# Two-layer attention kernel: value accumulators laid out by head and half of the queries

## The chip, the cores and the metric

One core of one Trainium2 chip runs the whole program. The metric is the device time of one execution in microseconds (us); the times shown are medians over several runs. The changed kernel does the same computation on the same inputs.

## What is computed

Two attention layers, A and B, are applied in turn, twice each, to one sequence of 2048 tokens of width 576, all in fp32. Both have 32 heads of 18 features; in A each head has keys and values of its own, in B all heads share one set.

```python
def _A_ref(x, wqkv, wo):
    qkv = ((x @ wqkv).reshape(B, S, 3, H, Dh)).transpose(2, 0, 3, 1, 4)
    q, k, v = qkv[0], qkv[1], qkv[2]
    scores = jnp.einsum("bhqd,bhkd->bhqk", q, k) * (Dh ** -0.5)
    p = _softmax(scores, axis=-1)
    o = jnp.einsum("bhqk,bhkd->bhqd", p, v)
    return o.transpose(0, 2, 1, 3).reshape(B, S, D) @ wo
# _B_ref: the same, with k and v of shape (B, S, Dh) shared by the heads
x = x + _A_ref(_layernorm(x), A_wqkv, A_wo)
x = x + _B_ref(_layernorm(x), B_wq, B_wk, B_wv, B_wo)
x = x + _A_ref(_layernorm(x), A_wqkv, A_wo)
x = x + _B_ref(_layernorm(x), B_wq, B_wk, B_wv, B_wo)
```

## The kernel before

A layer has a projection stage, a long stage of attention, and an output projection. Attention is worked in units: one pair of heads (p, 16 of them) by 512 queries (u, 4 of them), 64 units in a layer. Of a unit's 2048 keys, a head's scores are made twice.

First come the maxima. A matmul of kind "m" (line 653) gives the scores of 128 queries by 512 keys in a PSUM bank, and VectorE (DVE) reduces them (line 658). For four of the 32 in a unit the matmul takes the difference of two key blocks instead (kind "r", line 639), ScalarE (ACT) applies a relu (line 651), and DVE adds that while it reduces a later block (line 656), so that 28 reductions are left. The negated maxima go through GpSimd (POOL, lines 857 and 858), a DVE transpose (863) and DRAM (864, 868) into two rows of the query operand, so that the second score matmul has the maximum subtracted already.

Then come the exps. A matmul of kind "e" (line 879) gives 128 keys by 512 queries; ACT takes the exp into an SBUF tile `pt` (line 883). There are 32 in a unit, 16 of each head. The two heads of the pair lie on rows 0 to 63 and 64 to 127 of the array, so an "e", "m" or "r" of head 0 and one of head 1 can run side by side. All these matmuls share seven PSUM banks.

Last come the values. `pv_block` (line 913) multiplies four `pt` tiles, two key blocks of 128 by two heads, by the values: four matmuls with 19 columns of weights (18 features and a one, which gives the row sum) into four groups of 32 partitions of the one accumulator bank `oacc`, 512 queries wide. A group holds one head and either the even or the odd key blocks. A unit thus has 8 blocks of 512 columns, 4096 in all. fp32 makes two passes of each matmul.

When a unit's values are complete, ACT copies `oacc` to `oc` (line 930), and POOL adds the two key halves: `o_sum` (935) moves two groups and adds (939, 940) into `os`. Then the row sums are spread over 128 partitions by a DMA (`l_part`, 945), inverted on POOL (`l_inv`, 949), stored (`l_out`, 952), read back broadcast (`l_rows`, 957), multiplied on POOL (`o_mul`, 962) and the result is sent to `o_d` (`o_out`, 967). All DMAs go out on SyncE's queue (SP).

The order on TensorE (PE) in the steady stage is written out by hand in `UNIT` (line 70): ten phases of a unit. Each phase issues its rows in order ("e10" is kind, head and rank of the PSUM bank among the least recently used) and then a number of value columns, cut at block boundaries into segments. `PV_LAG` (line 81) says by how many columns the values trail: the first 928 columns of the first phases are left out. Maxima run 14 steps (`LEAD`; a step is four exps, an eighth of a unit) ahead of the exps, so 56 of a layer's 2048 maxima come before the loop of line 1044. After it the last exps go four by four (line 1060), with 512 value columns each, and parts of the output projection between.

The other steps of a unit are due at fixed distances, in steps, after its last exps (`SUM_AT` to `O_AT`, lines 50 to 57); `run_todo` issues what is due at the start of each phase.

Of the kernel before, what the change touches and what calls it, by code (L numbers as in the profile page):

```python
# [8 lines left out]
F32 = mybir.dt.float32  # L9
# [37 lines left out]
LEAD = 14  # L47
NM_AT = 2.5
ROW_AT = 5
SUM_AT = 3.75  # L50
L_AT = 5
INV_AT = 8
R_AT = 8
RB_AT = 11
MUL_AT = 13
O_AT = 15
SOON = (11.6, 12.6, 2.9)
FIRST = (8, 6)


# [6 lines left out]

UNIT = [("e00 m10 m02 e10 e01 e10 m00", 448),  # L70
# [9 lines left out]
UNIT = [([(o[0], int(o[1]), int(o[2])) for o in rows.split()], cols) for rows, cols in UNIT]  # L80
PV_LAG = 928
UNIT_M = [(kind, a) for rows, _ in UNIT for kind, a, _ in rows if kind != "e"]
assert len(UNIT_M) == 32 and sum(cols for _, cols in UNIT) == 4096

# [2 lines left out]
def tile_kernel(ctx: ExitStack, tc: tile.TileContext, A_x, A_wqkv, A_wo, B_x, B_wq, B_wk, B_wv, B_wo, out):  # L87
# [55 lines left out]
    r_d = dram.tile([H, S], F32, name="r_d")  # L143
    x_d = dram.tile([len(AWAY), P, D], F32, name="x_d")

    rb = cst.tile([P, 512], F32, name="rb")

    sums = [cst.tile([P, 512], F32, name=f"os{i}") for i in range(2)]

# [308 lines left out]
    for layer in range(4):  # L458
# [7 lines left out]
        def v_of(c):  # L466
            return vs[c // 8][:, c % 8] if is_a else vs[0][:, c]
# [113 lines left out]
                    fixed_rows(k_slot(p), True)  # L581
                load_rows(k_slot(p), D + 2 * p * DH, DH, 0, S, (i - 2,))

        mxs, nms, pts, ocs = {}, {}, {}, {}

        def ops(p):
            return big[:, q_slot(p)], big[:, k_slot(p)]
# [316 lines left out]
        def pv_cols(cols):  # L904

            while cols:
                n, c0 = divmod(pv_at[0], 512)
                w = min(cols, 512 - c0)
                pv_block(n, c0, c0 + w)
                pv_at[0] += w  # L910
                cols -= w

        def pv_block(n, c0, c1):

            p, u, i = *divmod(n // STEPS, 4), n % STEPS * 4
            cs = slice(c0, c1)
            turn[0] += 1
            for i in range(i, i + 4) if turn[0] % 2 else range(i + 3, i - 1, -1):
                a, kc = (i // 2) % 2, i // 4 * 2 + i % 2
                j = 64 * a + 32 * (kc % 2)  # L920
                nc.tensor.matmul(oacc[j:j + DH + 1, cs], v_of(kc)[:, 2 * p + a if is_a else 0, :], pts[p, u, i][:, cs],  # L921
                                 start=kc < 2 and c0 == 0, stop=kc >= 14 and c1 == 512)
                if c1 == 512:
                    pt = pts.pop((p, u, i))
                    free.extend(j for j, x in enumerate(ring) if x is pt)
            if c1 == 512 and i // 4 == STEPS - 1:
                oc = ocs[p, u] = ocs["tile"]
                ticks[0] += 1
                if m_done[0] < 4 * ns:
                    nc.scalar.activation(oc, oacc, AF.Copy)  # L930
                else:
                    copy(nc.vector, oc, oacc)


        def o_sum(p, u):
            oc = ocs.pop((p, u))
            t = sums[u % 2]
            for j in (0, 64):
                copy(nc.gpsimd, t[j:j + 32], oc[j + 32:j + 64])
            nc.gpsimd.tensor_tensor(t[:96], t[:96], oc[:96], op=OP.add)  # L940

        def l_part(p, u):
            lt = lts[p, u] = pool.tile([P, 8], F32, name="lt")
            for a in range(2):
                nc.sync.dma_start(lt[64 * a:64 * a + 64, :], sums[u % 2][64 * a + DH:64 * a + DH + 1, :])

        def l_inv(p, u):
            rl = rls[p, u] = pool.tile([P, 8], F32, name="rl")
# [5 lines left out]

        def l_rows(p, u):
            for a in range(2):
                nc.sync.dma_start(rb[64 * a:64 * a + DH, :],
                                  r_d[2 * p + a:2 * p + a + 1, u * 512:(u + 1) * 512].to_broadcast([DH, 512]))

        def o_mul(p, u):  # L960
            t = sums[u % 2]
            nc.gpsimd.tensor_tensor(t[:96], t[:96], rb[:96], op=OP.mult)  # L962

        def o_out(p, u):
            for a in range(2):
                c = (2 * p + a) * DH
                nc.sync.dma_start(o_d[c:c + DH, u * 512:(u + 1) * 512], sums[u % 2][64 * a:64 * a + DH, :])


        relu, raw = (pool.tile([P, 640], F32, tag="xh", bufs=2, name=n) for n in ("relu", "raw"))  # L970
# [17 lines left out]
        for p in range(NPAIR):  # L988
            for u in range(4):
                b = STEPS * (4 * p + u) + STEPS - 1  # L990
                if is_a or p or u:
                    at(b + NM_AT, max_store, p, u)
                    at(b + (SOON[2] if b == ns - 1 else ROW_AT), max_rows, p, u)
                soon = p == NPAIR - 1 and u == 0
                for d, f in ((SUM_AT, o_sum), (L_AT, l_part), (INV_AT, l_inv), (R_AT, l_out), (RB_AT, l_rows),
                             (SOON[0] if soon else MUL_AT, o_mul), (SOON[1] if soon else O_AT, o_out)):
                    at(b + LEAD + d, f, p, u)
            if p + 1 < NPAIR and is_a:
                for d, f in ((0, diff_in), (3, diff_split), (5, diff_out), (10 if p else 8, diff_rows)):
                    at(max(LEAD, 32 * p - 8) + d, f, p + 1)  # L1000
            if is_a and p in (0, 1):
                at(LEAD + 20 + 32 * p, load_rows, q_slot(p + 1), 2 * (p + 1) * DH, DH, 1536, S)
            if p + 1 < NPAIR:
                for i in range(4 if is_a else 2):
                    at(LEAD + 32 * (p - 1) + 1 + 8 * i if p else LEAD + 1 + 4 * i, load_part, p + 1, i)
# [15 lines left out]
                    f(*args)  # L1021

        b = LEAD + ns
        at(b - 9.75, out_rows, 0)
        at(b - 7, out_hi, 0, nc.vector)
        at(b - 6, out_lo, 0)
        at(b - 2, out_rows, 1)
        for i, (f, args) in enumerate(fill):
            if is_a and i % 8 == 0:
# [3 lines left out]
            f(*args)  # L1033
        assert not weave["left"] and m_done[0] == 4 * LEAD
        e_next = [0, 0]
        ocs["tile"] = ptile("oc")

        def exp_next(a, rank=0):
            pu, kc = divmod(e_next[a], NCH)
# [20 lines left out]
        while sum(e_next) < 4 * ns:  # L1060
            run_todo(LEAD + sum(e_next) / 4)
            for _ in range(min(4, 4 * ns - sum(e_next))):
                exp_next(int(e_next[0] > e_next[1]), next(i for i, j in enumerate(lru) if j not in held))
            left, c = 4 * ns - sum(e_next), -pv_at[0] % (512 * STEPS)
            if left < 4 * STEPS and 0 < c <= 512:
                pv_cols(c)
                for _ in range(FIRST[0]):
                    next(first)
                pv_cols(512 - c)
            else:  # L1070
                if left // 4 == 1:
                    for _ in range(FIRST[1]):
                        next(first)
                pv_cols(512)
        outs = out_proj(layer == 3, first)
        for st in range(ns, ns + L_AT + 1):
            run_todo(LEAD + st)
            if st < ns + OUT_AHEAD:
                next(outs)
                pv_cols(512 * ns - pv_at[0] - (0 if st > ns else 512))  # L1080
        tail = [todo.pop(n, []) for n in range(ns + LEAD + L_AT + 1, ns + LEAD + O_AT)]
        assert not todo, todo

# [30 lines left out]
```

## Time and profile before

| what | us |
|---|---|
| median of 3 runs | 5525.5 (5524.3 to 5525.83) |
| span of the profiled execution | 5520.9 |
| PE busy | 5509.2 |
| DVE busy | 4920.3 |
| ACT busy | 4889.3 |
| POOL busy | 1839.9 |
| weight loads (PEld) | 3050.7 |

Four layers follow one another, and each has about 1145 us of the steady stage. Busy times are unions of instructions: where instructions of one engine overlap, as ACT's, DVE's and PE's do here, a busy share near 100% does not say that the engine could do no more. What an engine could do is read from the time between the starts of two instructions that follow without a wait, and what bounds a stage from the time between the starts of its blocks.

### The profile page before, as it was taken

The numbers are of one execution on the slowest core, as the hardware profiler recorded it, in microseconds if no ns is written. First come the engines' busy times: TensorE is split into PE (matmuls) and PEld (weight loads), VectorE is DVE, ScalarE is ACT, GpSimd is POOL, SyncE is SP. The second block draws the span as 40 slices with busy tenths as digits, with TensorE's granted clock in tenths as the row PEclk, the third lists the DMA queues.
The fourth block names the chain that finished last, engine by engine and source line by source line (L and its number), as shares of the span: only waits on it lengthen the run. The fifth ranks groups of instructions, "written<-read, shape, count | busy, mean of one in ns | idle before, by whom it ended". The sixth has DMA issues, their size and how long they took to land.

```text
span 5520.9 us, 143086 instructions
## 1 busy us (share of the span) xinstructions
PE 5509.2 (100%) x55774; PEld 3050.7 (55%) x55774; DVE 4920.3 (89%) x9493; ACT 4889.3 (89%) x9882; POOL 1839.9 (33%) x2382
## 2 busy tenths in 40 slices
PE   9999999999999999999999999999999999999999
PEld 8655555454855555555686555545458545454546
DVE  4799999998799999999637999999977999999995
ACT  3599999999299999999626999999992999999996
POOL 3243333334233323233412433333342333333332
PEclk9999999999999999999999999999999999999999
DMA  6321111111411000001243211111114111010002
GB/s 219 119 60 45 45 45 48 43 45 34 136 57 31 24 24 21 24 21 25 64 176 109 58 49 43 45 46 48 40 43 133 54 28 25 24 25 21 24 15 84
DMA packets 277610, 306.04 MB, mean 55 GB/s; under 512 B 136434, under 2 KB 194378, under 8 KB 267642
## 3 DMA queue, kind: packets, MB, share of 16 engines
q1 hardware_dynamic: 276930, 296.89, 18.7%
q8 instruction: 437, 7.16, 0.5%
q14 instruction: 243, 1.99, 0.1%
HBM read 169.68 MB, written 123.13 MB: 53 GB/s over the span
## 4 chain that ended last, share of the span: by engine, by line
PE 97%; issue 1%; DVE 1%; ACT 1%; DMA 0%; POOL 0%; SPq 0%; POOLq 0%; ACTq 0%
PE oacc L921 38%; PE pse L879 27%; PE psm L653 17%; PE psn L275 7%; PE psq L481 5%; PE psm L639 3%; DVE mx L658 1%; ACT pt L883 1%; PE ps L261 0%; POOL ev L494 0%; DMA m_d<-tr 0%; DMA qk_d<-ev 0%; PE oacc L262 0%; DMA big<-m_d 0%; DMA big<-qk_d 0%
## 5 line engine op out<-in xcount | busy, mean ns | idle before, releaser
L883 ACT ACTIVATE pt<-pse 128x512 f32<-128x512 f32 x8192 | 4185.0, 612 | 10.1 <-PE pse L879 1.9
L658 DVE TENSOR_REDUCE mx<-psm 128x1 f32<-128x512 f32 x6208 | 3942.4, 684 | 88.6 <-PE psm L653 66.3
L879 PE MATMUL pse<-big 64*128 64x512 f32 x8192 | 2280.5, 432 | 0.5 <-DMA big<-m_d 0.5
L653 PE MATMUL psm<-big 62*128 62x512 f32 x7200 | 2158.9, 443 | 2.2 <-ACT evr L493 0.8
L879 PEld LDWEIGHTS pse<-big 64*128 64x128 f32 x8192 | 1174.4, 184 | 1064.2 <-ACT pt L883 758.2
L921 PE MATMUL oacc<-pt,vbuf 128*19 128x32 f32 (+11 forms) x26544 | 1728.2, 368 | 0.3 <-ACT oc L930 0.2
L653 PEld LDWEIGHTS psm<-big 62*128 62x128 f32 x7200 | 878.2, 184 | 204.3 <-DVE mx L658 75.9
L921 PEld LDWEIGHTS oacc<-pt,vbuf 128*19 128x19 f32 x26544 | 533.9, 98 | 819.9 <-issue 661.4
L186 POOL TENSOR_SCALAR hl<-neg 128x8 fp32r<-128x8 f32 x256 | 50.6, 198 | 2462.2 <-DVE neg L854 2462.2
L921 PE MATMUL oacc<-pt,vy 128*19 128x288 f32 (+3 forms) x8176 | 566.3, 383 | 0.0
L949 POOL TENSOR_TENSOR rl<-lt,mone 128x8 f32<-128x8 f32 x256 | 422.0, 1648 | 320.0 <-DMA lt<-os 318.1
L656 DVE CUSTOM_DVE_ANT_0 relu<-psm,relu 128x512 f32<-128x512 f32 x496 | 342.9, 691 | 76.3 <-ACT pt L883 50.9
L186 POOL TENSOR_SCALAR os<-oc 32x512 f32<-32x512 f32 x512 | 315.3, 616 | 102.4 <-DVE oc L186 50.6
L656 DVE CUSTOM_DVE_ANT_0 xo<-psm,xo 128x512 f32<-128x512 f32 x496 | 332.1, 670 | 15.5 <-ACT pt L883 1.6
L490 ACT ACTIVATE ev<-psq 128x512 fp32r<-128x512 f32 (+1 forms) x112 | 66.9, 597 | 311.5 <-PE psq L481 222.4
L940 POOL TENSOR_TENSOR os<-os,oc 96x512 f32<-96x512 f32 x256 | 330.6, 1291 | 21.4
L962 POOL TENSOR_TENSOR os<-os,rb 96x512 f32<-96x512 f32 x256 | 327.9, 1281 | 23.1 <-DMA rb<-r_d 23.1
L921 PEld LDWEIGHTS oacc<-pt,vy 128*19 128x19 f32 x8176 | 189.8, 98 | 242.0 <-issue 197.7
L651 ACT ACTIVATE xo<-psm 128x512 f32<-128x512 f32 x496 | 317.1, 639 | 0.0
L275 PE MATMUL psn<-wsm,xx 128*128 128x288 f32 x2240 | 310.4, 297 | 0.1
L275 PEld LDWEIGHTS psn<-wsm,xx 128*128 128x128 f32 x2240 | 299.0, 188 | 15.4 <-issue 13.1
L651 ACT ACTIVATE relu<-psm 128x512 f32<-128x512 f32 x496 | 303.6, 612 | 0.0
(102 smaller groups left out, 2781.3 us busy)
## 6 DMA issues: line engine op xcount, KB each, us to landing
big<-qk_d SPq DMA_DIRECT2D x172, 432.0 KB
qk_d<-ev SPq DMA_DIRECT2D x96, 512.0 KB
qk_d<-ev SPq DMA_DIRECT2D x120, 256.0 KB
rb<-r_d SPq DMA_DIRECT2D x512, 36.0 KB
o_d<-os SPq DMA_DIRECT2D x512, 36.0 KB
o<-o_d SPq DMA_DIRECT2D x56, 256.0 KB
xx<-qk_d SPq DMA_DIRECT2D x120, 72.0 KB
big<-m_d SPq DMA_DIRECT2D x512, 4.0 KB
```

The costliest lines, as they stand in the source:

```text
L186: eng.tensor_scalar(dst, src, 1.0, 0.0, op0=OP.mult, op1=OP.add)
L275: nc.tensor.matmul(ps, lhs[:, xc, :], wsm[:, wc, h * 288:(h + 1) * 288], start=i == 0, stop=i == len(TERMS) - 1)
L651: nc.scalar.activation(t, ps, AF.Relu)
L653: nc.tensor.matmul(ps, q[b:b + KM, c0:c0 + P], k[b:b + KM, kb * 512:(kb + 1) * 512], start=True, stop=True)
L656: nc.vector.tensor_tensor_reduce(t, ps, t, 1.0, LOWEST, OP.add, OP.max, mx[:, r:r + 1])
L658: nc.vector.reduce_max(mx[:, r:r + 1], ps, axis=AX.X)
L879: nc.tensor.matmul(e, k[r:r + KE, kc * P:(kc + 1) * P], q[r:r + KE, u * 512:(u + 1) * 512], start=True, stop=True)
L883: nc.scalar.activation(pt, e, AF.Exp, scale=SCALE)
L921: nc.tensor.matmul(oacc[j:j + DH + 1, cs], v_of(kc)[:, 2 * p + a if is_a else 0, :], pts[p, u, i][:, cs], start=kc < 2 and c0 == 0, stop=k ...
L940: nc.gpsimd.tensor_tensor(t[:96], t[:96], oc[:96], op=OP.add)
L949: nc.gpsimd.tensor_tensor(rl, lts.pop((p, u)), mone, op=OP.pow)
L962: nc.gpsimd.tensor_tensor(t[:96], t[:96], rb[:96], op=OP.mult)
```

## The change

The accumulator is divided otherwise: its four groups are two heads by two halves of the unit's queries. Each is 256 columns wide and sums over all keys, so `o_sum` and `oc` go, ACT copies 256 columns straight into `os`, and the later steps work on 128 partitions by 256 columns. A value block is one block of 128 keys: two `pt` tiles, each read in two halves, 16 blocks of 256 columns in a unit. The row sums are spread by one DMA in place of two, and the result is sent by four in place of two. The due steps after the sum lie one earlier. The table of ten phases is another one, with the same 32 e, 28 m and 4 r, and the values trail by 416 columns.

```diff
-SUM_AT = 3.75
-L_AT = 5
-INV_AT = 8
-R_AT = 8
-RB_AT = 11
-MUL_AT = 13
-O_AT = 15
-SOON = (11.6, 12.6, 2.9)
+L_AT = 4
+INV_AT = 7
+R_AT = 7
+RB_AT = 10
+MUL_AT = 12
+O_AT = 14
+SOON = (10.6, 11.6, 2.9)
...
-UNIT = [("e00 m10 m02 e10 e01 e10 m00", 448),
-        ("m10 e00 m11 m00 e10 e01", 480),
-        ("e10 m01 e00 m12 e10 m01", 320),
-        ("e10 e01 r10 m00", 256),
-        ("m00 m10 m00 e10 e02 r10", 480),
-        ("m10 e00 m12 m00 e11 e01 e10", 448),
-        ("e01 m10 e02 e10 r01 m11 m00", 416),
-        ("e10 m00 e10 e02 e10 m01 m10", 416),
-        ("e10 m00 e10 e02 e10 m01 m10", 416),
-        ("e00 m10 m00 m12 e00 r11 e00", 416)]
+UNIT = [("e02 m10 e12 m01 m12 e00", 416),
+        ("e10 e01 e01 m10 e10 m01", 384),
+        ("m11 m00 e10 m01 e00 e11", 448),
+        ("e00 m10 e01 m12 e00 e10 m00", 448),
+        ("e11 m02 m00 e10 e10 m01", 352),
+        ("e02 e10 m10 m01 e00 e10", 352),
+        ("m11 e01 m11 e00 r11 m00", 416),
+        ("e11 m00 e10 m10 r00 m10 e00", 416),
+        ("e02 m11 m02 e11 r00 e10 m00", 416),
+        ("m12 e02 m11 e01 e10 r01 m10", 448)]
...
-PV_LAG = 928
+PV_LAG = 416
...
-    rb = cst.tile([P, 512], F32, name="rb")
+    rb = cst.tile([P, 256], F32, name="rb")
...
-                n, c0 = divmod(pv_at[0], 512)
-                w = min(cols, 512 - c0)
+                n, c0 = divmod(pv_at[0], 256)
+                w = min(cols, 256 - c0)
...
-            p, u, i = *divmod(n // STEPS, 4), n % STEPS * 4
-            cs = slice(c0, c1)
+            p, u, kc = *divmod(n // NCH, 4), n % NCH
             turn[0] += 1
-            for i in range(i, i + 4) if turn[0] % 2 else range(i + 3, i - 1, -1):
-                a, kc = (i // 2) % 2, i // 4 * 2 + i % 2
-                j = 64 * a + 32 * (kc % 2)
-                nc.tensor.matmul(oacc[j:j + DH + 1, cs], v_of(kc)[:, 2 * p + a if is_a else 0, :], pts[p, u, i][:, cs],
-                                 start=kc < 2 and c0 == 0, stop=kc >= 14 and c1 == 512)
+            tiles = [(p, u, kc // 2 * 4 + 2 * a + kc % 2) for a in range(2)]
+            groups = [(a, h) for a in range(2) for h in range(2)]
+            for a, h in groups if turn[0] % 2 else groups[::-1]:
+                j = 64 * a + 32 * h
+                nc.tensor.matmul(oacc[j:j + DH + 1, c0:c1], v_of(kc)[:, 2 * p + a if is_a else 0, :],
+                                 pts[tiles[a]][:, 256 * h + c0:256 * h + c1],
+                                 start=kc == 0 and c0 == 0, stop=kc == NCH - 1 and c1 == 256)
...
-                    nc.scalar.activation(oc, oacc, AF.Copy)
+                    nc.scalar.activation(sums[u % 2][:, :256], oacc[:, :256], AF.Copy)
...
-        def o_sum(p, u):
-            oc = ocs.pop((p, u))
-            t = sums[u % 2]
-            for j in (0, 64):
-                copy(nc.gpsimd, t[j:j + 32], oc[j + 32:j + 64])
-            nc.gpsimd.tensor_tensor(t[:96], t[:96], oc[:96], op=OP.add)
...
-            for a in range(2):
-                nc.sync.dma_start(lt[64 * a:64 * a + 64, :], sums[u % 2][64 * a + DH:64 * a + DH + 1, :])
+            nc.sync.dma_start(lt, sums[u % 2][DH::32, :256])
...
-                nc.sync.dma_start(rb[64 * a:64 * a + DH, :],
-                                  r_d[2 * p + a:2 * p + a + 1, u * 512:(u + 1) * 512].to_broadcast([DH, 512]))
+                src = r_d[2 * p + a, u * 512:(u + 1) * 512].rearrange("(h t) -> h t", h=2)
+                nc.sync.dma_start(rb[64 * a:64 * a + 64, :], src[:, None, :].to_broadcast([2, 32, 256]))
...
-            t = sums[u % 2]
-            nc.gpsimd.tensor_tensor(t[:96], t[:96], rb[:96], op=OP.mult)
+            t = sums[u % 2][:, :256]
+            nc.gpsimd.tensor_tensor(t, t, rb, op=OP.mult)
...
-                nc.sync.dma_start(o_d[c:c + DH, u * 512:(u + 1) * 512], sums[u % 2][64 * a:64 * a + DH, :])
+                for h in range(2):
+                    j, t0 = 64 * a + 32 * h, u * 512 + 256 * h
+                    nc.sync.dma_start(o_d[c:c + DH, t0:t0 + 256], sums[u % 2][j:j + DH, :256])
...
-        at(b - 9.75, out_rows, 0)
-        at(b - 7, out_hi, 0, nc.vector)
-        at(b - 6, out_lo, 0)
+        at(b - 10.75, out_rows, 0)
+        at(b - 8, out_hi, 0, nc.vector)
+        at(b - 7, out_lo, 0)
...
-            left, c = 4 * ns - sum(e_next), -pv_at[0] % (512 * STEPS)
+            left, c = 4 * ns - sum(e_next), -pv_at[0] % (256 * NCH)
...
-                pv_cols(512 * ns - pv_at[0] - (0 if st > ns else 512))
+                pv_cols(max(0, 512 * ns - pv_at[0] - (0 if st > ns else 256)))
```

## Rows read from the trace of the kernel before

**Rows 1.** The page: span, busy times by engine, the chain that ended last.

```profile
span 5520.9 us, 143086 instructions
...
PE 5509.2 (100%) x55774; PEld 3050.7 (55%) x55774; DVE 4920.3 (89%) x9493; ACT 4889.3 (89%) x9882; POOL 1839.9 (33%) x2382
...
PE 97%; issue 1%; DVE 1%; ACT 1%; DMA 0%; POOL 0%; SPq 0%; POOLq 0%; ACTq 0%
```

**Rows 2.** Stretch table, one turn: length, busy us of PE, PEld, DVE, ACT, POOL.

```profile
1001.54:1019.93 18.39, 18.39 (x202) 9.23 (x200) 17.74 (x35) 18.37 (x38) 5.79 (x7) 1.00 0.13 32
```

**Rows 3.** Timeline of PE in that turn: start, length, engine, line, operation, tiles, shape, count.

```profile
1001.54 1.00 PE L921 MATMUL oacc<-pt,vy 128*19 128x480 f32 x8
1002.47 0.50 PE L879 MATMUL pse<-big 64*128 64x512 f32 x1
...
1003.37 0.73 PE L921 MATMUL oacc<-pt,vbuf 128*19 128x320 f32 x8
1004.04 0.50 PE L879 MATMUL pse<-big 64*128 64x512 f32 x2
...
1004.72 0.63 PE L921 MATMUL oacc<-pt,vbuf 128*19 128x192 f32 x16
1005.28 0.50 PE L653 MATMUL psm<-big 62*128 62x512 f32 x2
1005.62 0.40 PE L879 MATMUL pse<-big 64*128 64x512 f32 x1
...
1006.18 1.01 PE L921 MATMUL oacc<-pt,vbuf 128*19 128x448 f32 x16
...
1007.12 0.49 PE L879 MATMUL pse<-big 64*128 64x512 f32 x1
...
1008.25 0.95 PE L921 MATMUL oacc<-pt,vbuf 128*19 128x448 f32 x8
1009.13 0.50 PE L879 MATMUL pse<-big 64*128 64x512 f32 x1
...
1016.99 0.50 PE L879 MATMUL pse<-big 64*128 64x512 f32 x1
...
1019.93 1.00 PE L921 MATMUL oacc<-pt,vy 128*19 128x480 f32 x8
```

**Rows 4.** Timeline of ACT in the same turn.

```profile
1002.66 0.60 ACT L930 ACTIVATE oc<-oacc 128x512 f32<-128x512 f32 x1
...
1006.08 1.10 ACT L883 ACTIVATE pt<-pse 128x512 f32<-128x512 f32 x2
...
1007.69 3.55 ACT L883 ACTIVATE pt<-pse 128x512 f32<-128x512 f32 x7
```

**Rows 5.** Stretch table of the exps (line 883) alone, at the end of the first layer.

```profile
1353.00:1369.00 16.00, 16.00 (x35) 1.00 0.26 67
```

**Rows 6.** Timeline of DVE in the turn of rows 3.

```profile
1008.32 1.28 DVE L658 TENSOR_REDUCE mx<-psm 128x1 f32<-128x512 f32 x2
```

**Rows 7.** Groups by line and form, whole span: busy us, mean ns; idle before.

```profile
L883 ACT ACTIVATE pt<-pse 128x512 f32<-128x512 f32 x8192 | 4185.0, 612 | 10.1 <-PE pse L879 1.9 <-PE psm L653 1.8
L658 DVE TENSOR_REDUCE mx<-psm 128x1 f32<-128x512 f32 x6208 | 3942.4, 684 | 88.6 <-PE psm L653 66.3
L921 PEld LDWEIGHTS oacc<-pt,vbuf 128*19 128x19 f32 x26544 | 533.9, 98 | 819.9 <-issue 661.4 <-ACT oc L930 91.2
L839 ACT ACTIVATE vbuf<-psn 128x288 f32<-128x288 f32 x32 | 13.2, 412 | 45.2 <-PE psn L275 45.2
L254 ACT ACTIVATE xx<-oacc 128x128 fp32r<-128x128 f32 x31 | 8.8, 285 | 0.0
```

**Rows 8.** Waits of SP's queue, 400 to 1290 us: who for whom, total, times, longest.

```profile
SPq L864 <- DVE mx L656: 437.5, 49, 11.4
```

**Rows 9.** Timeline of SP and of POOL in the turn of rows 3.

```profile
1010.72 0.52 SPq L868 DMA_DIRECT2D big<-m_d  x2
...
1011.01 1.64 POOL L949 TENSOR_TENSOR rl<-lt,mone 128x8 f32<-128x8 f32 x1 [1.42 <-DMA lt<-os]
```

More of the change, by code (lines that the diff above doesn't have):

```diff
@@ L582, in load_part @@
                 load_rows(k_slot(p), D + 2 * p * DH, DH, 0, S, (i - 2,))
-        mxs, nms, pts, ocs = {}, {}, {}, {}
+        mxs, nms, pts = {}, {}, {}
         def ops(p):
@@ L913, in pv_block @@
         def pv_block(n, c0, c1):
-            p, u, i = *divmod(n // STEPS, 4), n % STEPS * 4
-            cs = slice(c0, c1)
+            p, u, kc = *divmod(n // NCH, 4), n % NCH
             turn[0] += 1
-            for i in range(i, i + 4) if turn[0] % 2 else range(i + 3, i - 1, -1):
-                a, kc = (i // 2) % 2, i // 4 * 2 + i % 2
-                j = 64 * a + 32 * (kc % 2)
-                nc.tensor.matmul(oacc[j:j + DH + 1, cs], v_of(kc)[:, 2 * p + a if is_a else 0, :], pts[p, u, i][:, cs],
-                                 start=kc < 2 and c0 == 0, stop=kc >= 14 and c1 == 512)
-                if c1 == 512:
-                    pt = pts.pop((p, u, i))
+            tiles = [(p, u, kc // 2 * 4 + 2 * a + kc % 2) for a in range(2)]
@@ new lines, in pv_block @@
+            groups = [(a, h) for a in range(2) for h in range(2)]
[4 more added lines that the diff above has]
+                                 start=kc == 0 and c0 == 0, stop=kc == NCH - 1 and c1 == 256)
+            if c1 == 256:
+                for t in tiles:
+                    pt = pts.pop(t)
@@ L925, in pv_block @@
                     free.extend(j for j, x in enumerate(ring) if x is pt)
-            if c1 == 512 and i // 4 == STEPS - 1:
-                oc = ocs[p, u] = ocs["tile"]
+            if c1 == 256 and kc == NCH - 1:
                 ticks[0] += 1
                 if m_done[0] < 4 * ns:
-                    nc.scalar.activation(oc, oacc, AF.Copy)
+                    nc.scalar.activation(sums[u % 2][:, :256], oacc[:, :256], AF.Copy)
                 else:
-                    copy(nc.vector, oc, oacc)
@@ L935, in o_sum @@
-        def o_sum(p, u):
-            oc = ocs.pop((p, u))
-            t = sums[u % 2]
-            for j in (0, 64):
-                copy(nc.gpsimd, t[j:j + 32], oc[j + 32:j + 64])
-            nc.gpsimd.tensor_tensor(t[:96], t[:96], oc[:96], op=OP.add)
+                    copy(nc.vector, sums[u % 2][:, :256], oacc[:, :256])
         def l_part(p, u):
             lt = lts[p, u] = pool.tile([P, 8], F32, name="lt")
-            for a in range(2):
-                nc.sync.dma_start(lt[64 * a:64 * a + 64, :], sums[u % 2][64 * a + DH:64 * a + DH + 1, :])
+            nc.sync.dma_start(lt, sums[u % 2][DH::32, :256])
@@ L994, in tile_kernel @@
                 soon = p == NPAIR - 1 and u == 0
-                for d, f in ((SUM_AT, o_sum), (L_AT, l_part), (INV_AT, l_inv), (R_AT, l_out), (RB_AT, l_rows),
+                for d, f in ((L_AT, l_part), (INV_AT, l_inv), (R_AT, l_out), (RB_AT, l_rows),
                              (SOON[0] if soon else MUL_AT, o_mul), (SOON[1] if soon else O_AT, o_out)):
@@ L1035, in tile_kernel @@
         e_next = [0, 0]
-        ocs["tile"] = ptile("oc")
         def exp_next(a, rank=0):
```

## The prediction

> **What bounds the kernel now.** I read the page first: TensorE (PE) is busy all of the 5520.9 us, and the chain that ended last lies on it for 97% [rows 1]. A modelled PE busy time proves little, since its matmuls overlap, so the next view is the table by stretches: in the stage that repeats, one turn of the table takes 18.39 us, with PE busy 18.39, ScalarE (ACT) 18.37 and VectorE (DVE) 17.74 [rows 2]. Three engines look full. The reader is to see that two of them are not: their instructions overlap, and a late one stretches the busy time without filling it.
>
> ACT: at the layer's end, where exps follow one another and PE waits, 35 exps touch 16.00 us [rows 5]; one alone lasts 0.61 [rows 7], so about 1.3 are in flight at any instant, and the pace is 0.48 us from start to start. A turn has 32 exps, 4 relus and one copy: 36 x 0.48 + 0.50 = 17.8 us of 18.39. DVE: two reductions in a row take 1.28 us and one takes 0.68, so 0.60 from start to start [rows 6, 7]; 28 of them and some 0.5 for small ones are 17.3 us. Both have 0.6 to 1.1 us of slack in a turn.
>
> PE: the timeline gives it without modelled ends, from start to start of its two kinds of block [rows 3]. A block of score matmuls depends on how many rows of a phase fall on one head, for the two heads lie on different rows of the array and start together: a phase with at most 2 rows on a head takes 0.68 us (1004.04 to 1004.72), with 3 rows 0.90 (1002.47 to 1003.37, 1005.28 to 1006.18), with 4 rows 1.13 (1007.12 to 1008.25). That is 0.23 + 0.225 per slot. A value block takes cols/0.6 ns + 0.133 us: 480 columns 0.93, 320 columns 0.67, 448 columns 0.88 in one segment; 256 columns cut in two segments 0.56. So a further segment costs some 0.005 us. Counting the old table: its ten phases have 4, 3, 3, 2, 3, 4, 4, 4, 4, 4 slots, 35 in all, and 4096 columns in 17 segments. The turn is 10 x 0.23 + 35 x 0.225 + 6.83 + 10 x 0.133 + 7 x 0.005 = 18.37 us against 18.39 seen. PE is the bound, almost without waits.
>
> **The change part by part.**
>
> *The table.* Rows by head in the new phases: 3, 3, 3, 4, 3, 3, 3, 4, 4, 4, that is 34 slots: the 64 rows (32 exps, 28 maxima, 4 relus) are the same, but six phases instead of four share out evenly. One slot less: -0.225 us.
>
> *Value blocks by head and half.* 4096 columns remain, and four column groups remain: 2 heads x 2 halves instead of 2 heads x 2 keys. The boundaries now lie every 256 columns, so a turn is cut in 23 segments, not 17: 6 x 0.005 = +0.03 us. Their unseen price is bounded by nothing and by the 0.1 us of one weight load of this line [rows 7] a segment; I take the value blocks' row, since it holds whole segments. That two streams now read two halves of one tile has no row; I take zero, as each of the four still has its own columns, and leave it to the rivals.
>
> *The copy of the accumulator.* On ACT, 512 columns took 0.60 us [rows 4]; 256 must lie between 0.28 (128 columns) and 0.41 (288) [rows 7], about 0.39, so ACT gets 0.21 us back and its load falls to 17.6 us a turn of some 18.2: its slack stays. PE's next value block waits for this copy: now the blocks end near 1002.47, the copy runs 1002.66 to 1003.26 and the value block starts at 1003.37 [rows 3, 4], covered by a 3-slot block with 0.1 to spare. The new turn ends before phase 2, also 3 slots, so 0.3 to spare.
>
> *The sum on POOL goes,* and the division is over 256 columns; POOL is busy 5.79 of 18.39 us [rows 2], so nothing on the path. The copy now writes the buffer that the result is sent from, so ACT could wait for an old transfer, with all exps behind it: the result is sent in step 14 of the unit, the buffer is overwritten near step 17.8; 3.8 steps of 2.3 us (an eighth of a turn) are 8.7 us, against 0.26 us for an issue [rows 9] and a landing that no row gives. Nothing, unless it lands after more than 8 us, which would show as late copies.
>
> *SP.* One DMA fewer for the row sums, two more for the result, all moved a step earlier. SP waits for DVE before the maxima's store for 437.5 us in 49 turns, 8.9 us a turn [rows 8], so one issue more, 0.26 us by the maxima's loads [rows 9], is hidden. One order turns: the reciprocals' store, which waits for a POOL instruction of 1.64 us, will stand before the maxima's two loads. In the old kernel these go out at 1010.72, and the next unit's exps, which need them, start at 1016.99 [rows 3, 9]: 6.3 us cover the 1.64 and a store, with 4 left for the landing. If that cover were gone, each turn would pay the lateness in full.
>
> *Values trail by 416 columns instead of 928.* This is the part that can cost. A first exp of a phase ends 1.07 to 1.18 us after its matmul starts: matmul 1005.62, exp 1006.08; matmul 1007.12, exp 1007.69 [rows 3, 4]; and 0.61 for itself [rows 7]. In the old table, a value segment that needs an exp of its own phase comes only in phase 10, 1.13 + 0.53 = 1.66 us after it: 0.5 to spare. In the new one, three do so early. Phase 2's last segment (128 columns) needs its first row: 0.90 + 256/0.6 ns = 1.33 us, 0.15 to 0.26 to spare; phase 5 the same; phase 3's last 64 columns need its second pair, 0.34 later: 0.90 + 0.64 - 0.34 = 1.20, 0.02 to 0.13 to spare. The phases before these have 3, 4 and 4 ACT instructions in 1.7 to 2.0 us, 0.48 each, so ACT is not behind when they start, or by a hair. I take zero; between zero and 0.1 at each of the three is the bound without a backlog.
>
> *The layer's ends.* There ACT runs its exps without a pause [rows 5] and sets the pace of the last 14 groups. What the values no longer trail is done at the start of the loop instead. Nothing either way.
>
> *Sum.* -0.225 + 0.03 = -0.195 us a turn. Of 2048 maxima of a layer 56 come before the loop, so 1992/32 x 4 = 249 turns: -48.6 us. On the profiled 5520.9 that gives 5472; the median stands 4.6 above that span, so 5477.
>
> [...] The blocks with two segments show that the weights of the second come in under the first: 256 columns in two segments carry the same 0.13 us as 448 in one [rows 3]. [...]
>
> **The rivals.**
> 1. *Weight loads show.* With six more segments of two passes, each exposing its 0.098 us load [rows 7], a turn grows by 1.2 - 0.225 = 0.95 us: 5762. Against it stand the rows above; the same sign would follow if two halves of one tile could not stream side by side. 3%.
> 2. *The values catch up with the exps.* Mechanism: PE takes instructions in order, so a segment that waits for its exp holds the next phase's matmuls, and so ACT's next work. If ACT is one exp (0.48) behind at the ends of phases 2, 3 and 5, the three waits are 0.27 + 0.4 + 0.27 = 0.94 us, a turn 0.75 longer: 5712. It decides against the change from 0.195 us of waits a turn on. For it: margins of 0.02 to 0.26 where the old smallest was 0.5. Against: no phase before them leaves a backlog. 9%.
> 3. *Banks eat a part.* Seven PSUM banks serve 64 rows a turn; a shorter turn reuses them sooner, and the row order is new. The old turn has 0.02 to 0.1 us of such waits (18.37 against 18.39, or the scatter of its 4-slot blocks). Another 0.1 with a little waiting for values leaves -0.09: 5503. 15%.
> 4. *No change that shows.* ACT or DVE takes over: DVE's 17.3 us is the nearest, 0.9 below; with waits of 0.15 to 0.24 a turn the time is within 5514 to 5537. 8%.
>
> **How the numbers follow.** The forecast, -0.13 to -0.28 us a turn (the upper end with the old waits gone too), 5456 to 5493, has 65%, and 5477 is its sum. With rival 3 the range goes to 5510; 5458 to 5510 then holds some 8 in 10. Faster by over 0.2% (11 us, about what a measurement of this kernel can tell) is the forecast and rival 3: 0.80; within it rival 4: 0.08; slower rivals 1 and 2: 0.12.
>
> **What the profile after would show.** Right: copies of the accumulator every 18.2 us and 0.39 us long; 3-slot blocks of 0.90 and 4-slot blocks of 1.13; value blocks of three segments at cols/0.6 + 0.14; POOL's additions gone. Wrong: value blocks of phases 2, 3 and 5 longer than their columns (rival 2); each segment dearer (rival 1); score blocks above 0.90 and 1.13 with weight loads that wait for ACT or DVE (rival 3); a turn at DVE's or ACT's own count (rival 4).

## The result: 14 us slower, not 49 us faster

The kernel after takes 5539.28 us (5534.76 to 5543.84) against 5524.9 us (5522.9 to 5526.15) of the kernel before: a ratio of 1.0027 [1.0018, 1.0035]. The forecast was 5477 us. The page of after (answers [rows 1]), its profiled execution being 5538.54 us:

```profile
span 5536.8 us, 167817 instructions
...
PE 5513.2 (100%) x68222; PEld 3451.4 (62%) x68222; DVE 4939.9 (89%) x9493; ACT 4847.7 (88%) x9882; POOL 1044.5 (19%) x1614
...
PE 96%; issue 1%; DVE 1%; DMA 1%; POOL 1%; ACT 1%; SPq 0%; ACTq 0%; POOLq 0%
```

The stretch table of one turn (answers [rows 2], columns as there):

```profile
818.20:836.61 18.41, 18.41 (x250) 10.80 (x249) 17.85 (x35) 18.20 (x38) 5.99 (x9) 1.00 0.15 30
```

TensorE (PE) is still the chain, at a granted clock of 1.00 in that turn. Work went away (POOL 795 us less, ACT 42 us less), and PE did one slot of score matmuls less in a turn, but the turn is as long as before. The time from one copy of the accumulator to the next has a median of 18.384 us before and 18.402 after. Three places together make 14.2 of the 15.9 us between the two spans:

| place | how counted | us |
|---|---|---|
| the ordinary turn | 249 x (18.402 - 18.384) | +4.5 |
| turns off the median, above all a few dear (long) ones | excess over the median, summed over 244 intervals between copies: 9.98 against 3.20 | +6.8 |
| the ends of three layers | last copy of a layer to first of the next: 202.79, 308.42, 202.75 against 201.68, 307.64, 201.75 | +2.9 |

The other 1.7 us lie in the start and in the last layer's end.

**The ordinary turn.** The timeline of PE in phases 5 to 7 (start, length, engine, line, operation, tiles, shape, count; answers [rows 3]):

```profile
823.18 0.50 PE L878 MATMUL pse<-big 64*128 64x512 f32 x1
...
823.77 0.49 PE L652 MATMUL psm<-big 62*128 62x512 f32 x1
824.20 0.79 PE L920 MATMUL oacc<-pt,vbuf 128*19 128x256 f32 x16
824.92 0.50 PE L878 MATMUL pse<-big 64*128 64x512 f32 x2
...
825.81 0.79 PE L920 MATMUL oacc<-pt,vbuf 128*19 128x160 f32 x16
826.53 0.49 PE L652 MATMUL psm<-big 62*128 62x512 f32 x1
826.65 0.49 PE L878 MATMUL pse<-big 64*128 64x512 f32 x1
...
827.57 0.31 PE L920 MATMUL oacc<-pt,vbuf 128*19 128x64 f32 x8
```

All three are blocks of 3 slots, for which 0.90 us was forecast. Phase 6 takes that (824.92 to 825.81). Phase 5 takes 1.02 (823.18 to 824.20) and phase 7 1.04 (826.53 to 827.57). The weight loads (PEld) tell where:

```profile
823.52 0.18 PEld L878 LDWEIGHTS pse<-big 64*128 64x128 f32 x1
823.77 0.18 PEld L652 LDWEIGHTS psm<-big 62*128 62x128 f32 x1
...
826.53 0.18 PEld L652 LDWEIGHTS psm<-big 62*128 62x128 f32 x1 [0.32 <-issue]
826.65 0.18 PEld L878 LDWEIGHTS pse<-big 64*128 64x128 f32 x1
```

In phase 7 the first two rows belong to different heads. The first two of phase 5 do too, and start within 0.01 us of each other (823.18 and 823.19); here the second comes 0.12 us later. In phase 5 the load for the last row starts only at 823.77, with the matmul, instead of under the matmul before it. Both wait for a PSUM bank that is still read, as the timelines of VectorE (DVE) and ScalarE (ACT) show:

```profile
819.88 3.15 DVE L657 TENSOR_REDUCE mx<-psm 128x1 f32<-128x512 f32 x5
822.95 0.18 DVE L853 TENSOR_REDUCE neg<-mx 128x8 f32<-128x32 f32 x1
823.04 0.68 DVE L657 TENSOR_REDUCE mx<-psm 128x1 f32<-128x512 f32 x1
823.73 0.21 DVE L862 STREAM_TRANSPOSE tr<-hl 128x32 f32<-128x32 f32 x1
823.86 6.40 DVE L657 TENSOR_REDUCE mx<-psm 128x1 f32<-128x512 f32 x10
...
817.93 0.40 ACT L930 ACTIVATE os<-oacc 128x256 f32<-128x256 f32 x1
...
825.51 3.04 ACT L882 ACTIVATE pt<-pse 128x512 f32<-128x512 f32 x6 [0.21 <-PE pse L878]
```

Followed through the bank ranks of `UNIT`, phase 5's last row (m01) takes the bank of phase 4's last maximum, and phase 7's second row (e01) that of phase 6's second exp. The reduction that holds phase 5's bank ends at 823.72, 0.05 us before the load. Ahead of it stands a negation that does not belong to it, and DVE has had no pause over 0.1 us since 819.88. For phase 7, the second of the six exps ends about 826.60 (825.51, one start-to-start time of 0.48, and 0.61 for itself), again 0.05 before the load. ACT was not behind there: it had waited 0.21 us for PE before these exps (end of its row), but the bank came free 1.68 us after its matmul started (824.92 to 826.60), and phase 7 could have used it after 1.61 (826.53). The median of the 46 turns between 400 and 1240 us has the same 0.05 us in both places. Over those turns the median block exceeds 0.23 + 0.225 per slot by 0.109 us in phase 5, 0.127 in phase 7 and 0.025 in phase 3; all others are within 0.005. Before, no phase exceeded it by more than 0.017.

**A dear turn.** The timelines of SP, POOL and PE (answers [rows 9]):

```profile
1284.36 0.56 SPq L863 DMA_DIRECT2D m_d<-tr  x1
...
1293.72 0.58 SPq L943 DMA_DIRECT2D r_d<-rl  x1
1294.35 0.79 SPq L867 DMA_DIRECT2D big<-m_d  x2
...
1290.40 0.41 POOL L185 TENSOR_SCALAR big<-raw 128x256 fp32r<-128x256 f32 x1 [5.37 <-DMA raw<-in_B_wk_dram]
...
1292.05 1.65 POOL L940 TENSOR_TENSOR rl<-lt,mone 128x8 f32<-128x8 f32 x1
...
1296.33 0.47 PE L878 MATMUL pse<-big 64*128 64x512 f32 x1 [1.53 <-DMA big<-m_d]
```

The maxima's rows (`big<-m_d`) stand behind the reciprocals' store (`r_d<-rl`) on SP. That store waits for POOL, and POOL first splits weights of the next layer, for which it waited 5.37 us. So the rows go out 10 us after the maxima's store, and PE stands. Before, the rows went out ahead of the reciprocals' store, 7.3 us after the maxima's (1283.59 and 1290.89):

```profile
1290.89 0.55 SPq L868 DMA_DIRECT2D big<-m_d  x2
1294.80 0.60 SPq L952 DMA_DIRECT2D r_d<-rl  x1
```

Of 244 turns four take 19.7 us or more: from 1278 and 4040 us near a layer's end, where weights for the next layer come in, from 2988 at a layer's start, where POOL first makes key differences (begun at 2998.08, after 4.54 us of waiting for their data), and from 4061. In the first three the rows go out right behind the reciprocals' store, 9.2 to 10.9 us after the maxima's store, and PE waits 1.5, 2.4 and 1.9 us for them. In the fourth they are not late (3.5 us); it follows straight on the one of 4040 and is long in its first blocks, and it goes with the other three in `max_rows_first` below.

**A layer's end.** PE's timeline there:

```profile
1356.86 0.73 PE L878 MATMUL pse<-big 64*128 64x512 f32 x4
1357.52 1.38 PE L920 MATMUL oacc<-pt,vbuf 128*19 128x192 f32 x24
1358.83 0.73 PE L878 MATMUL pse<-big 64*128 64x512 f32 x4
1359.49 1.35 PE L920 MATMUL oacc<-pt,vbuf 128*19 128x192 f32 x24
```

A block of 512 columns takes 1.28 to 1.31 us from start to start instead of the 0.99 of before: trailing by 416 columns, its last segment of 64 needs exps of its own group.

### The profile page after: what moved, and what is told of

Read it like the earlier page. It is cut to its first block, busy times and chain, and to the rows that moved or that the text cites. A ratio compares the mean times of both kernels' runs of the same rounds, so it can differ in the third digit from the quotient of the medians.

```text
span 5536.8 us, 167817 instructions
## 1 busy us (share of the span) xinstructions
PE 5513.2 (100%) x68222; PEld 3451.4 (62%) x68222; DVE 4939.9 (89%) x9493; ACT 4847.7 (88%) x9882; POOL 1044.5 (19%) x1614
## 3 DMA queue, kind: packets, MB, share of 16 engines
q14 instruction: 239, 1.96, 0.1%
## 4 chain that ended last, share of the span: by engine, by line
PE 96%; issue 1%; DVE 1%; DMA 1%; POOL 1%; ACT 1%; SPq 0%; ACTq 0%; POOLq 0%
PE oacc L920 37%; PE pse L878 27%; PE psm L652 16%; PE psn L274 7%; PE psq L480 6%; PE psm L638 3%; DVE mx L657 1%; PE ps L260 0%; ACT pt L882 0%; POOL ev L493 0%; DMA big<-m_d 0%; DMA m_d<-tr 0%; PE oacc L261 0%; DMA xx<-qk_d 0%; POOL rl L940 0%
## 5 line engine op out<-in xcount | busy, mean ns | idle before, releaser
L878 PE MATMUL pse<-big 64*128 64x512 f32 x8192 | 2420.3, 440 | 8.7 <-DMA big<-m_d 6.6
L652 PE MATMUL psm<-big 62*128 62x512 f32 x7200 | 2389.1, 432 | 2.4 <-ACT evr L492 1.4
L920 PE MATMUL oacc<-pt,vbuf 128*19 128x256 f32 (+5 forms) x35872 | 1743.3, 315 | 2.6 <-ACT pt L882 0.8
L920 PEld LDWEIGHTS oacc<-pt,vbuf 128*19 128x19 f32 x35872 | 842.3, 98 | 799.6 <-issue 462.9
L652 PEld LDWEIGHTS psm<-big 62*128 62x128 f32 x7200 | 1126.5, 184 | 305.3 <-issue 138.8
L920 PE MATMUL oacc<-pt,vy 128*19 128x256 f32 (+3 forms) x11296 | 571.7, 323 | 1.3 <-ACT pt L882 0.4
L920 PEld LDWEIGHTS oacc<-pt,vy 128*19 128x19 f32 x11296 | 266.3, 98 | 221.4 <-issue 131.2
L495 DVE TENSOR_TENSOR ev<-psq,ev 128x512 fp32r<-128x512 f32 (+1 forms) x84 | 58.0, 691 | 206.3 <-ACT ev L489 193.0
L638 PE MATMUL psm<-big 54*128 54x512 f32 x512 | 225.2, 440 | 0.0
L638 PE MATMUL psm<-xx,big 54*128 54x512 f32 x480 | 211.7, 441 | 0.0
```

The lines of the kernel that those rows point to most:

```text
L638: nc.tensor.matmul(ps.rearrange("p (h t) -> p h t", h=2) if p == 0 or not is_a else ps, q[b:b + 3 * DH, c0:c0 + P], k, start=True, stop=True)
L652: nc.tensor.matmul(ps, q[b:b + KM, c0:c0 + P], k[b:b + KM, kb * 512:(kb + 1) * 512], start=True, stop=True)
L878: nc.tensor.matmul(e, k[r:r + KE, kc * P:(kc + 1) * P], q[r:r + KE, u * 512:(u + 1) * 512], start=True, stop=True)
L920: nc.tensor.matmul(oacc[j:j + DH + 1, c0:c1], v_of(kc)[:, 2 * p + a if is_a else 0, :], pts[tiles[a]][:, 256 * h + c0:256 * h + c1], start ...
```

## The experiments

All are edits of the kernel after. Where a turn is given, it is the median time between copies of the accumulator; block times are medians of the turns between 400 and 1240 us, from the start of a block's first matmul to that of the next block.

**Are the late blocks waits for readers of banks?** `half_readers` halves what reductions and exps read, and so leaves out half of the maxima and of the exps.

```diff
-                    nc.vector.reduce_max(mx[:, r:r + 1], ps, axis=AX.X)
+                    nc.vector.reduce_max(mx[:, r:r + 1], ps[:, :256], axis=AX.X)
...
-            nc.scalar.activation(pt, e, AF.Exp, scale=SCALE)
+            nc.scalar.activation(pt[:, :256], e[:, :256], AF.Exp, scale=SCALE)
```

> The changed kernel, but every reduction of the maxima reads 256 of its bank's 512 columns, and every exp makes 256 of 512 columns (the value matmuls read the first half twice): it leaves out half of the maxima and of the exps. All TensorE instructions stay as they are. Theory banks (the saved slot is given back because the score matmuls of phases 5 and 7 wait for PSUM banks that VectorE and ScalarE still read): the score blocks of phase 5 (1.01 us) and phase 7 (1.03) fall to the 0.90 of the other 3-slot blocks, phase 3 from 0.93 to 0.90, the turn from 18.40 to 18.15 us, the span by 249 x 0.25 = 62 us to some 5475. Theory layout (TensorE itself is slower with two halves of one tile or with more segments): the blocks and the turn stay, 18.40. Theory values (blocks wait for exps because the values trail less): value blocks carry 0.137 over their columns now, and nothing there can fall.

Measured, in one run: turn 18.112 us, 5446.58 us in all against 5526.1 of before. Phases 3, 5 and 7 fall to 0.902, 0.893 and 0.898, PE's work being the same, and the turn is even 0.05 below the 18.16 to which slots, columns and segments add up. So all that the turn has over these is waiting for readers. The value blocks' part beyond columns stays at 1.38 us a turn: it is the segments, not a wait for exps.

**Which reader?** `half_max` and `half_exp` make the two halves of that edit alone.

> The kernel after, but the reductions of the maxima read 256 of the 512 scores of a bank; the exps stay whole. It leaves half of the maxima out. This splits the run in which both readers were halved (turn 18.11 us, blocks of phases 3, 5 and 7 at 0.90). If each late block waits for the reader that the trace names, phases 5 and 3 (banks read by the reductions) fall from 1.014 and 0.930 to 0.90, phase 7 (a bank read by an exp) stays at 1.03, and the turn falls from 18.41 to about 18.27. Rival: the readers delay each other through the common order of the banks, then all three blocks fall with the maxima alone and the turn is near 18.15.

> The kernel after, but the exps read and write 256 of the 512 scores of a bank, and the values use those twice; the reductions stay whole. It leaves half of the exps out. If each late block waits for the reader that the trace names, phase 7 falls from 1.032 to 0.90, phase 5 stays at 1.01, and the turn falls from 18.41 to about 18.28. Rival: ACT's pace as a whole holds the turn, then all blocks fall and the turn is near 18.12; or the reductions alone, then phase 7 stays too and the turn stays at 18.40.

Measured, in one run each: turns 18.283 and 18.281, 5503.14 and 5492.36 us. PE's timeline of `half_max` in phases 5, 6 and 7, then of `half_exp` in phases 5 and 7:

```profile
819.70 0.50 PE L878 MATMUL pse<-big 64*128 64x512 f32 x1
...
820.60 0.79 PE L920 MATMUL oacc<-pt,vbuf 128*19 128x256 f32 x16
821.32 0.50 PE L878 MATMUL pse<-big 64*128 64x512 f32 x2
...
822.30 0.79 PE L920 MATMUL oacc<-pt,vbuf 128*19 128x160 f32 x16
```

```profile
818.86 0.50 PE L878 MATMUL pse<-big 64*128 64x512 f32 x1
...
819.89 0.79 PE L920 MATMUL oacc<-pt,vbuf 128*19 128x256 f32 x16
...
822.23 0.49 PE L652 MATMUL psm<-big 62*128 62x512 f32 x1
822.23 0.49 PE L878 MATMUL pse<-big 64*128 64x512 f32 x1
```

With short reductions phase 5 is at 0.90 (819.70 to 820.60), median 0.894; with short exps it stays at 1.03, median 1.015, while phase 7's first two rows start together again, median 0.920. So phase 5 is DVE's and phase 7 is ACT's, as the loads said. Two details came out otherwise: phase 3 is ACT's (0.934 and 0.904), and with short reductions a new wait of 0.08 appears in phase 6 (821.32 to 822.30) while phase 7 falls to 0.950. When PE comes sooner, it meets ACT sooner; part of what is saved goes to the next reader. Phases 6 and 7 together take 1.93 us in the kernel after, in `half_max` and in every later run that keeps its table, and only shorter exps bring them to 1.82 or less: the wait moves between the two, but it is ACT's.

**Is it the values that trail less?** `trail_more` changes PV_LAG from 416 to 1248 and the ring of `pt` tiles from 14 to 15.

> The changed kernel with the values trailing by three phases (1248 columns) instead of one (416), and 15 exp tiles in the ring instead of 14. Theory values: the score and value blocks of phases 3, 5 and 7 lose their extra, turn 18.15, 60 us less. Theory banks: phases 5 and 7 keep 1.01 and 1.03, turn 18.40; only the layer's end, where value blocks wait 0.3 us each for exps of their own group, gains about 1 us a layer: 4 us less in all, or nothing if the longer tail of values after the last exp takes it back.

Measured: turn 18.443, 5544.32 us (ratio 1.0034 [1.0021, 1.0046]). The turn is 0.04 longer and nothing comes back, so values waiting for exps cost nothing in the loop. The waits move (0.104 in phase 5, 0.117 in 6, 0.030 in 8, 0.020 in 9), perhaps because other columns now lie at the copy: that is the author's reading, which no run shows.

**Layout or table?** `old_table` keeps the new accumulators and puts the old `UNIT` and PV_LAG = 928 back.

> The new layout with the old table of ten phases and the values trailing by 928 columns again. Theory banks: the layout itself costs only its segments, 25 against 17 in a turn at some 0.005 us, so the turn is 18.38 + 0.03 = 18.41, no block longer than in the kernel before, and the layer's end is as before; time within 0.2% of the kernel before, +5 us. Theory layout: phases come out longer than their slots, turn above 18.5, time above 5550.

Measured: turn 18.414, 5541.11 us (1.0028 [1.0016, 1.0039]). The layout alone costs 0.03 us a turn: 8 further segments are 0.04. One phase (7) did grow, to 1.166, against the expectation. The time is some 15 us above that of before, not 5: irregular turns are 9 of it (an excess of 12.17 us against 3.20). Dear turns are there with either table (here 22.8 and 22.7 us), so they do not come from the table.

**The dear turns.** `max_rows_first` takes the maxima's rows out from behind the reciprocals' store:

```diff
-ROW_AT = 5
+ROW_AT = 4.75
```

> The changed kernel with the maxima's two loads due a quarter step earlier (4.75 instead of 5), so that they stand before the reciprocals' store in the queue, as in the kernel before. If the long turns of the changed kernel (20.0, 20.4, 21.0, 19.7 us) come from these loads standing behind a store that waits for POOL, TensorE's 6.6 us of waiting for them goes, and with it 6 to 9 us of the span; the usual turn stays at 18.40. If they come from something else, the long turns stay.

Measured: 5530.0 us (1.0009 [1.0000, 1.0017]), 9 us less than after (8.3 by the two spans). PE's waits for these rows (total, times, longest), in the kernel after and then in this run, and SP's timeline of this run at the place shown above:

```profile
PE pse L878 <- DMA big<-m_d: 6.6, 5, 2.4
```

```profile
PE pse L878 <- DMA big<-m_d: 2.3, 3, 1.3
```

```profile
1290.52 0.55 SPq L867 DMA_DIRECT2D big<-m_d  x2
1293.92 0.57 SPq L943 DMA_DIRECT2D r_d<-rl  x1
```

The rows go out 3.8 us sooner, the excess of irregular turns falls from 9.98 to 1.21 us, and no turn is dear any more. So the dear turns came from these due steps.

**The layers' ends.** `end_trails_rows_first` keeps that edit and leaves the values out of the first group after the loop, so that they trail by 928 columns there.

```diff
-                pv_cols(512)
+                pv_cols(512 - held_back)
+                held_back = 0
```

> The kernel after with two edits: the maxima's rows go out a quarter of a step earlier (ROW_AT 4.75, alone 5530.0), and the first group behind the loop leaves its 512 value columns out, so that the values trail by 928 columns at a layer's end. If the last groups' value segments that wait for exps of their own group cost about 1.07 us a layer net, this gives back 4 us: about 5526, no turn in the steady stage changes. Rival: what the tail's groups lose is covered, since ACT sets their pace: 5530. Against both: the 512 columns move behind the last exp, where nothing covers them, and cost 4 x 0.85 us: 5533.

Measured: 5525.07 us (1.0000 [0.9991, 1.0009]), 5 us less again. Against the kernel before as it ran beside each, it is 3.3 us; the two spans differ by 3.5, the ends of three layers together by 3.2 (711.12 against 714.29). Its timeline of PE at the place shown above:

```profile
1356.12 1.74 PE L878 MATMUL pse<-big 64*128 64x512 f32 x8
1357.79 1.07 PE L920 MATMUL oacc<-pt,vbuf 128*19 128x192 f32 x24
1358.79 1.04 PE L878 MATMUL pse<-big 64*128 64x512 f32 x4
1359.76 1.06 PE L920 MATMUL oacc<-pt,vbuf 128*19 128x192 f32 x24
```

In these first groups nothing is won: 1.96 us a group against 1.97, which the author puts down to ACT's pace: in the kernel after 35 exps from 1353.91 take 17.37 us in a row, 1.97 for four. The gain is later, where ACT has caught up: after the woven output projection (1371.9 us) its next two groups take 1.66 and 1.74 us, those of after 1.90 and 1.97. There the wait for exps holds up PE: in the kernel after the load at 1375.28 comes after 0.61 us of idle time, which an exp ends. And PE then holds up ACT: the first exps of two groups start 0.60 us after their group's first matmul (1374.15 and 1378.07), 0.51 and 0.56 after the exp ahead of them, where most others start 0.48 apart.

**Other tables.** Three tables came from a walk on paper through PE's blocks, the seven banks, and the queues of ACT and DVE. `other_table`: 35 slots, PV_LAG 768; `table_c`: 35 slots, 832; `table_d`: 35 slots, 448. (The expectation of `table_d` says 34, but its fifth phase has four rows on one head, and its score block takes 1.157 us: by the formula a 4-slot block, not a 3-slot block.) Two phases of `other_table`:

```diff
+        ("m01 e13 e00 r10 m11 m01 r10", 448),
+        ("m12 e00 m10 m00 e00 e10 e00", 288)]
```

> The kernel after with another table, ROW_AT 4.75 and the values trailing by 768 columns. Its phases have 3, 3, 3, 3, 3, 4, 4, 4, 4, 4 slots, 35 in all, one more than the table of after, but rows and bank ranks were chosen so that no weight load should meet a bank that is still read. If waits for banks are what the table of after lost, the turn is formula alone: 18.37 from the slots plus 0.03 for the segments, down to 18.30 where blocks hide a little; 5500 to 5530. Rival: the waits come back elsewhere, as with the old table in the new layout (phase 7 at 1.166, turn 18.414): 5530 to 5545.

Measured: 5664.72 us (1.0253 [1.0239, 1.0267]), turn 18.948, of which the last phase's score block has 0.455 over its slots. Its weight loads and ACT there:

```profile
1023.05 0.18 PEld L878 LDWEIGHTS pse<-big 64*128 64x128 f32 x1 [0.51 <-ACT relu L650]
...
1022.40 0.60 ACT L650 ACTIVATE relu<-psm 128x512 f32<-128x512 f32 x1 [0.38 <-PE pse L878]
```

A relu comes late, and its bank with it. The profile names PE as what released it, but the relu's matmul was long done (started 1020.70); DVE's last read of the buffer that this relu overwrites ended at 1022.30, 0.1 us before it. That the relu waited for this read is inferred from these times. This wait was not in the walk, and was added for the next two.

> The layout of after, ROW_AT 4.75, values trailing by 832 columns, and a table of 35 slots whose order and ranks were worked out by a walk through banks, ACT and DVE with the durations of the traces, this time with the wait of a relu for its buffer (the term whose absence the run other_table showed). The walk gives it 0.08 us a turn less than the table of after: about 18.33 us and, without the dear turns and with the values trailing at the layer's ends, 5505. If waits for readers can't be ordered away because ACT and DVE are near their own pace, the turn is again 18.38 to 18.45 and the time 5518 to 5535; if the walk lacks a further wait, the turn is longer than 18.5.

> The layout of after with ROW_AT 4.75 and the end of the layers trailing by 512 columns more, as in end_trails_rows_first (5525.07), values trailing by 448 columns, and another table with 34 slots, found by the same walk: 0.04 us a turn less than the table of after, that is 18.37 us and 5515. If the slot that is saved always comes back as waits for readers, the turn stays at 18.38 to 18.45 and the time at 5518 to 5535.

Measured: 5537.58 us (1.0023 [1.0014, 1.0033]), turn 18.446, and 5619.69 us (1.0171 [1.0154, 1.0188]), turn 18.784. In `table_c` waits are only some 0.05 us a turn, but it has the 35th slot; in `table_d` one block of three slots is 0.29 late. The walk missed both. So no second table of 34 slots was run, and whether another one would do better is not shown.

**DVE's small steps.** In the kernel after, the negation of a unit's maxima (0.09 us from its start to the next one's) and its transpose (0.13) stand on DVE just where phase 5's bank is due: in all 46 turns the negation right ahead of the reduction that holds it, the transpose right behind. `neg_after_three` builds on `end_trails_rows_first` and moves both behind those reductions; `neg_after_six` moves them further (6 and 3.5).

```diff
-NM_AT = 2.5
+NM_AT = 3.25
...
-            while m_full and i >= m_full[0][1] + 2:
+            while m_full and i >= m_full[0][1] + 3:
```

> The kernel end_trails_rows_first (5525.07 us) with DVE's two small steps moved: the negation of a finished unit's maxima comes after the third reduction past the unit's end instead of the second, and its transpose one phase later (phase 6). In the kernel after, DVE works without a pause from 819.88 to 834.74, and these two steps, 0.09 and 0.13 us, stand just ahead of the reduction whose bank phase 5 waits for. If they are what makes it late, phase 5 falls from 1.014 to 0.91 to 0.93, some 0.04 come back in phase 6, and with less lateness handed on the turn is 18.33 us: about 5506. If the work of the reductions as a whole makes the bank late, a shift of 0.22 us moves the wait to another phase: turn 18.38 to 18.42, 5520 to 5530. Slower, if the later transpose makes the maxima's rows late for the next unit's exps: turns above 18.6.

> As neg_after_three, but the negation after the sixth reduction past the unit's end and the transpose in phase 7, behind all reductions of phases 5 and 6. If the place ahead of phase 5's reductions is what costs, phase 5 falls to 0.92, and phase 8 (reductions after the moved steps) gains up to 0.05: turn 18.33, about 5506. If the wait only moves, phase 6, 7 or 8 takes it over in full and the turn stays at 18.38 to 18.42: 5520 to 5530. The maxima's rows go out two phases after the transpose's store, so late rows are likelier than in neg_after_three.

Measured: 5503.94 us (0.9961 [0.9947, 0.9974]) and 5505.33 us (0.9964 [0.9951, 0.9976]), turns 18.313 in both. DVE's timeline in `neg_after_three`, then PE's in phases 6 and 7:

```profile
820.37 0.18 DVE L853 TENSOR_REDUCE neg<-mx 128x8 f32<-128x32 f32 x1
820.57 1.89 DVE L657 TENSOR_REDUCE mx<-psm 128x1 f32<-128x512 f32 x3
822.37 0.20 DVE L862 STREAM_TRANSPOSE tr<-hl 128x32 f32<-128x32 f32 x1
...
821.66 0.50 PE L878 MATMUL pse<-big 64*128 64x512 f32 x2
...
822.60 0.79 PE L920 MATMUL oacc<-pt,vbuf 128*19 128x160 f32 x16
```

Phase 5 falls from 1.014 to 0.922, phase 7 from 1.032 to 0.979, and 0.05 comes back in phase 6 (0.94 here): 0.09 us a turn for 0.22 us of DVE work put 0.6 and 1.8 us later. Phases 6 and 7 together stay as they were, so the gain is phase 5's, and it is as large as the negation, which alone stood ahead of its bank; the two steps were not moved one by one. This version is 0.4% faster than the kernel before, and faster than the one after.

## Why the prediction was wrong, step by step

- **The slot: right.** -0.225 us a turn. Blocks without a wait follow the formula within 0.005 us after, and all blocks of before within 0.017; with the readers halved the whole turn comes to 18.112 against the 18.16 of the sum.
- **The segments: right.** +0.03 forecast; the value blocks' part beyond columns grew from 1.352 to 1.381 us. The rival by which each weight load shows is out: a further segment costs 0.005 us. The rival counted 0.196, two loads of 0.098; a segment of four value matmuls does show as eight matmuls and eight loads (x8 at 827.57), two of each a matmul, but their time does not show.
- **The copy and the sum on POOL: right.** The copy takes 0.40 us (forecast 0.39), and POOL's additions are gone. Neither was on the path, so neither pays.
- **Values that trail less: right in the loop.** None of the three tight segments waits; `trail_more` brings nothing back.
- **Banks: the step that failed.** Rival 3 had the mechanism, but priced it at "another 0.1"; it is 0.109 + 0.127 + 0.025 = 0.26 us a turn, and so takes the whole 0.195 and a little more. The wrong step is in the first part: "Both have 0.6 to 1.1 us of slack in a turn" is a mean over the turn. A reduction is on PE's path when PE wants its bank, and DVE runs 15 us of the turn (819.88 to 834.74) with no pause over 0.1 us, so there the slack is nothing and a step of 0.09 us in DVE's order shows in PE. On ACT it is not the load either: the way from a matmul through its exp to the free bank (1.68 us) is longer than the 1.61 us that the table leaves between phases 6 and 7. Counts of work decided that DVE and ACT are not the bound; the order in which banks come free had no row in the argument. `neg_after_three` shows it most plainly: same work, other place, 0.09 us a turn. Rival 4, a turn at DVE's or ACT's own count, is out: by the prediction's counts that would be 17.3 or 17.6 us, not 18.40.
- **SP's order: priced at nothing, 8 to 9 us.** "6.3 us cover the 1.64 and a store" holds in nearly all turns. It was read from one turn, and failed in those where POOL had other work before the reciprocals, for whose data it waited some 5 us. The prediction said that "each turn would pay the lateness in full" if the cover went; a handful did.
- **The layers' ends: "Nothing either way", 3 to 5 us.** Values that trail by 416 columns wait in each last group. The forecast looked at the columns that had to be done, not at which exps the last 64 of them need; it had checked this for the loop alone.

In sum: 53 us of the missing 64.5 (between the forecast of -48.6 and +15.9 in span) are the turn, 249 x (0.195 + 0.018), and most of the rest the two priced at nothing. The two undone bring the kernel to the time before, and with DVE's two steps moved it lies 21 us below. The slot's other part, the waits of phases 6 and 7, stays open: together these phases take 1.93 us against 1.81 by the formula, and no order tried here got rid of that.

## What to carry to other kernels

Where three engines share a few buffers and each is over nine tenths busy (here PE 18.41, ACT 18.20 and DVE 17.85 of 18.41 us), removing work from the slowest one is worth what the others' next release allows, not what it takes off (here 0.26 us a turn of waits against a slot of 0.225); before counting a saved slot, ask of each buffer when its last reader will end, at the new times. A small step of an engine costs by its place (0.09 us a turn for DVE's two): look at what stands just ahead of the instruction that releases the scarce buffer. And a cover that is read from one ordinary turn (the 6.3 us here) holds for that turn only; look for the turn in which the same queue has other work.

## What the runs showed of the hardware

- A weight load that found its bank free was hidden under the matmul before it (in the kernel after 0.18 us from 823.52, under the 0.39 of a matmul that started at 823.52; its own started at 823.76); where the bank came free late, the matmul started with its load (823.77 and 823.77), and the block of 0.90 us took 1.02: 0.05 us passed from the end of the reader to the start of the load, with DVE (823.72 to 823.77) as with ACT (826.60, worked out above, to 826.65).
- PE took its blocks in the order of issue there: behind the last score matmul of phase 5, late at 823.77, the value columns started at 824.20, 1.02 us after the phase's first row instead of 0.90.
- Halving a reduction's columns brought it from 0.684 to 0.420 us, halving an exp's from 0.612 to 0.387 (`half_readers` against the kernel after): an estimate by a straight line through the two gives a fixed part of 0.16 us each. The copy of the accumulator went from 0.60 in the kernel before to 0.40 in the one after, by the same estimate with a fixed part of 0.20: half its columns took two thirds of the time.
